# Moving the bulk transfers of an attention and MLP kernel from SyncE's queue to ScalarE's

## The chip, the cores and the metric

The kernel runs on one core of a Trainium2 chip. The core has TensorE (PE in the profile), VectorE (DVE), ScalarE (ACT), GpSimd (POOL) and SyncE (SP); each has its own instruction stream, worked off in order, and transfers between HBM and SBUF are issued as instructions in such a stream (SP's or ACT's here) and carried by 16 DMA engines. The metric is the device time of one launch in microseconds, as the median over runs.

## The reference

A layer of 2048 tokens of width 512, in float32: a layernorm without learned scale, from which an attention of 32 heads of 16 and a GELU MLP of width 1792 both read; their outputs and the input are added.

```python
xn = _layernorm(x)                                   # [1, 2048, 512]
qkv = (xn @ wqkv)                                    # 32 heads, Dh = 16
p = softmax(einsum("bhqd,bhkd->bhqk", q, k) * 16 ** -0.5)
a = einsum("bhqk,bhkd->bhqd", p, v).reshape(1, 2048, 512) @ wo
m = gelu(xn @ w1 + b1) @ w2 + b2                     # tanh form, F = 1792
return x + a + m
```

## The kernel before

**Units.** The attention is cut into 8 groups of 4 heads (NG) and 4 blocks of 512 queries (NQB), so 32 pairs t, and each pair into 16 units, one for each 128 keys. A unit is about 2.6 us long and does three things for different pairs: `s_half` makes four score tiles for a coming pair (PE, banks `pS`) whose row maxima DVE takes (L402); `e_half` makes four transposed score tiles of the present pair with the maxima folded in as two more rows of the product (PE, `pT`, three PSUM banks in turn), and ACT takes their exponentials into `pe` (L443, 12 buffers); `v_half` multiplies these with the values (PE, `pV`). There are 2048 exponentials. Between these products PE works on a list of background products (`dense`, banks `pD`): projections of values, queries and keys, then the MLP's two products, then the output projection. All of PE's products stand at one line of the program, L174.

**Stages.** The first 88 us are a start-up plan (layernorm, the first projections). From 88 to about 330 us the background is the rest of the projections, and GpSimd splits weights into pairs of float16 numbers, which are stored to HBM scratch. From about 330 to 1300 us it is the MLP in four blocks of 512 tokens, and then, to the end, the output projection.

**Transfers.** The background brings and keeps its data by transfers of its own: weight chunks in halves of 256 KB (`wch`, L887), columns for the projections (`wq`, L622); the normalised input `xt`, stored to scratch `xn_d` in 16 pieces (L1296) and read back as `xb`, 4 pieces for each block of the MLP (L709); the first MLP weight as 56 blocks `wc` of 256 KB (L714, three buffers, fetched two groups ahead); the second as 14 pieces into `w2_s` (L1425); and the partial sums `ac` (L1487). The attention has smaller ones, all on SP: stores of projected queries and keys (`qk_d`, L659 and L660), their loads as `kst` and `qst` (L565), the maxima as rows of `qst` (L360 and L364), and, at the end of each pair t, a chain for the sums of the softmax: `den_d` from `osb` (L494), back as `dn` (L497), its inverse to `den_d` (L504), spread as `rb` (L508), and the finished output `ot_d` (L520).

**What sets the order.** The program's order is the hardware's order on each of the five engines (`manual_schedule` with ORDERED). `later(n, fn, local, bulk)` puts a step in a queue that is due n ticks later; `tick`, called as the units go on, emits what is due. Steps with a size in `bulk` go through a lane that emits them at a limited rate:

```python
def run_lane(all_of_them=False):
    credit[0] = min(credit[0], 0) + LANE          # LANE = 225
    while lane and (all_of_them or credit[0] > 0 and not held[0]):
        size, fn = lane.pop(0)
        credit[0] -= size
        fn()
```

So the place of a transfer among all other instructions is the place in the program at which `fn` runs, whichever engine issues it. Each transfer counts up one of eight completion semaphores, taken in turn over all transfers of the program whatever engine issues them (DMAHW0 to DMAHW7 in the order below). Before it is issued its engine waits for the transfer eight back, which has the same semaphore, unless it is known to have landed; further waits are for data and for buffers.

Of the kernel before, what the change touches and what calls it, by code (L numbers as in the profile page):

```python
# [18 lines left out]
P = 128  # L19
S = 2048  # L20
D = 512
# [5 lines left out]
NF = F // P  # L27
QB = 512
# [16 lines left out]
WFROM, WSTEP, XN = 10, 4.5, 4.5  # L45
# [13 lines left out]
def layer_kernel(ctx: ExitStack, tc: tile.TileContext, x, wqkv, wo, w1, b1, w2, b2, out):  # L59
    nc = tc.nc  # L60
# [14 lines left out]
    xn_d = dram.tile([P, 2, NC, S], F16, name="xn_d")  # L75
    w1_d = dram.tile([NF // 2, P, 2, 2, NC, P], F16, name="w1_d")
    w2_d = dram.tile([P, 2, NF, D], F16, name="w2_d")
    acc_d = dram.tile([S, D], F32, name="acc_d")
# [143 lines left out]
    class Plan:  # L222
# [7 lines left out]
        def add(self, engine, ns, fn, after=(), take=(), free=(), size=0, tail=0, gap=0, small=False, lag=0):  # L230
            t = dict(gap=gap, small=small, lag=lag, e=engine, ns=ns, fn=fn, after=[a for a in after if a], take=take, free=free, size=size, tail=tail,
                     end=None, n=len(self.todo))
            for key in free:
                self.users.setdefault(key, []).append(t)
            self.todo.append(t)
            return t
# [66 lines left out]
    def later(n, fn, local=False, bulk=0):  # L303
        queue.append((slot[0] + n, fn, local, bulk))
# [262 lines left out]
    def stacks(g, w, blocks):  # L567
        for b in blocks:
            for a in range(2):
                stack(g, w, b, a)  # L570
# [45 lines left out]
    def load_qk(m):  # L616
        wf = []
        for w in range(2):
            wf.append(ph.tile([P, D], F32, name="wq", bufs=2).rearrange("p (c n) -> p c n", n=P))

            def load(w=w):
                nc.sync.dma_start(wf[w], wqkv[:, w * D + m * P:w * D + (m + 1) * P].rearrange("(c p) n -> p c n", p=P))  # L622
                here[m, w] = slot[0] + 4

            later(0, load, True, 256)
        return wf
# [12 lines left out]
    def by_slots(gen):  # L639

        def step():
            w = FINE
            while w == FINE:
                w = next(gen, 0)
            if w is None:
                later(1, step, True)

        later(1, step, True)
# [54 lines left out]
    feed, xbs, wcs = [], {}, {}  # L703

    def fetch_x(b):
        if b < NQB:
            xbs[b] = feed[0].tile([P, 2, NC, QB], F16, name="xb", bufs=1)
            for c in range(NC):
                later(1 + c, lambda c=c: nc.sync.dma_start(xbs[b][:, :, c], xn_d[:, :, c, b * QB:(b + 1) * QB]))  # L709

    def fetch_w1(n):
        if n < NQB * NF:
            wcs[n] = feed[0].tile([P, 2, NC, P], F16, name="wc", bufs=3)
            nc.sync.dma_start(wcs[n], w1_d[n % NF // 2, :, n % 2])  # L714

    def group(gen):

# [155 lines left out]
    with ExitStack() as st1:  # L873
# [3 lines left out]
        xt = ph.tile([P, 2, NC, S], F16, name="xt")  # L877
        xs = {}

        def chunk(src):  # L880
            wf = ph.tile([P, 4 * W], F32, name="wch", bufs=3)
            v = wf.rearrange("p (a b) -> p a b", b=src.shape[2])
            n = src.shape[1] // 2
            got = [v, 0, 0]

            def half(r):
                nc.sync.dma_start(v[:, r], src[:, r])  # L887
                got[1] += 1
                got[2] = pos[0] + 2

            for a in range(2):
                later(2, lambda r=slice(n * a, n * a + n): half(r), True, 256)
            return got
# [273 lines left out]
        for w in (1, 0):  # L1167
            wf, hi, lo, i1 = ("wq", 0, w), wqh[:, w, 0], wqh[:, w, 1], inv0[:, w:w + 1]
# [22 lines left out]
        for i in range(2):  # L1191
# [6 lines left out]
            else:  # L1198
                b = add("POOL", 1240, lambda key=key: nc.gpsimd.tensor_scalar(
                    tl[key], tl[key], inv_v[:, 0:1], 0.0, op0=ALU.mult, op1=ALU.add), [h])  # L1200
# [90 lines left out]
        def rest():  # L1291
            for k in range(8):
                later(8 + 4 * k, lambda k=k: stacks(1, 1 - k // 4, [k % 4]), True, 192)
            for k in range(4 * NQB):
                c, cols = k % 4, slice(k // 4 * QB, k // 4 * QB + QB)
                later(int(10 + XN * k), lambda c=c, cols=cols: nc.sync.dma_start(xn_d[:, :, c, cols], xt[:, :, c, cols]), True, 256)  # L1296
            for t in range(NV, NT):
                yield v_group(t, wvh, dbank)
            yield project(0, 0, NQB - 1, wqh, dbank)
            for m in range(1, 4):  # L1300
                while m not in ready_w:
                    yield None
                if m < 3:
                    by_slots(split_qk(m + 1, wfs[m + 1], inv1[0], ready_w))
                for sb in range(NQB):
                    for w in (1, 0):
                        yield project(m, w, sb, ready_w[m], dbank)
                    if m == 3 and sb == 2:
                        for n in range(2):
                            fetch_w1(n)  # L1310
                        fetch_x(0)
# [78 lines left out]
    def mlp():  # L1390
        m2 = st2p
        w2_s = m2.tile([P, 2, NF, D], F16, name="w2_s")
# [24 lines left out]
        for b in range(NQB):  # L1417
            xb = xbs[b]
            g = m2.tile([P, 2, NF, QB], F16, name="g", bufs=1)
            for f in range(NF):  # L1420
                later(1, lambda n=b * NF + f + 2: fetch_w1(n))
                wc = wcs[b * NF + f]
                if b == 0 and f >= 3:
                    for k in range(f - 3, NF if f == NF - 1 else f - 2):
                        later(2 * (k - f + 3), lambda k=k: nc.sync.dma_start(w2_s[:, :, k], w2_d[:, :, k]))  # L1425
                if b == 0 and f == 3:
                    nc.sync.dma_start(b2_b, b2[None, :].to_broadcast([P, D]))

                def hidden(hp, g=g, b=b, f=f):
                    hh = m2.tile([P, QB], F32, name="hh", bufs=3)  # L1430
                    bias = b1_s[:, f:f + 1]
                    if f % 2 == 0:
                        h_scale[0] = scale_reg(f"hs{f // 2 % 2}", fac1[0][0:1, f // 2:f // 2 + 1])
                    scale = h_scale[0]
                    nc.scalar.activation(hh, hp, AF.Identity, scale=scale, bias=bias)  # L1435
                    given("act", 700)
                    later(1, lambda: gelu(hh, g, b, f), True)

                yield Group([lambda c=c, i=i, j=j, wc=wc, xb=xb: (wc[:, i, c, :], xb[:, j, c, :])
                             for c in range(NC) for i, j in PAIRS], dbank, hidden, pace=FAST if f % 2 else SLOW)  # L1440
            for q in range(4):
                t = b * 4 + q
                xa = m2.tile([P, D], F32, name="xa", bufs=2)
                if q == 1:
                    fetch_x(b + 1)
                if b == NQB - 1 and q == 1:

                    ocs[2] = feed[0].tile([P, 2, NC, QB], F16, name="xb", bufs=1)
                    when((NG - 2) * NQB + 2, lambda: read_o(ocs[2], 2, True), 2)
                    for k in range(3):  # L1450
                        acs[8 + k] = feed[0].tile([P, D], F32, name="ac", tag="wc", bufs=3)
                        later(3 + k, lambda k=k: read_acc(acs[8 + k], 8 + k))
                nc.sync.dma_start(xa, x[t * P:(t + 1) * P, :])
                later(3, lambda xa=xa: pooled((1280, lambda: nc.gpsimd.tensor_tensor(xa, xa, b2_b, op=ALU.add))), True)

                def store(yp, xa=xa, t=t):
                    yt = m2.tile([P, D], F32, name="yt", bufs=2)
                    nc.scalar.activation(yt, yp, AF.Copy, scale=scale_reg("ys", gs[0:1, 2:3]))  # L1458
                    given("act", 600)
                    add = lambda: nc.gpsimd.tensor_tensor(xa, xa, yt, op=ALU.add)  # L1460
                    put = lambda: nc.sync.dma_start(acc_d[t * P:(t + 1) * P, :], xa)
                    later(1, lambda: pooled((1280, add), (0, lambda: later(4, put, True))), True)

                yield Group([lambda f=f, i=i, j=j, q=q, g=g: (g[:, i, f, q * P:(q + 1) * P], w2_s[:, j, f, :])
                             for f in range(NF) for i, j in PAIRS], dbank, store,
                            lambda n, b=b: (b, n // 3) in done, pace=FAST if b > 1 else MEAN)
# [17 lines left out]
        later(0, lambda: later(2, then), False, 1)  # L1484

    def read_acc(ac, t):
        later(0, lambda: nc.sync.dma_start(ac, acc_d[t * P:(t + 1) * P, :]), False, 256)  # L1487

    def finish(ac, t, store, *yos):
        put = lambda: nc.sync.dma_start(out[t * P:(t + 1) * P, :], ac)  # L1490
# [129 lines left out]
```

## Time and profile before

| | us |
|---|---|
| median of 3 runs | 1439.21 (1437.81 to 1444.19) |
| the profiled execution | 1438.07 |
| its span, first to last instruction | 1436.3 |
| DVE busy, mostly row maxima (L402, 1279.1) | 1346.9 |
| POOL busy | 693.4 |

The profile is of one execution; its time is 1.8 us above its span. A row of the page's groups gives the line of the program, the engine and operation, the tile written and the tile read, the count, the busy time and the mean duration, and what ended the engine's idle time ahead of it. A timeline row gives the start and length in us; a row with "x4" is four instructions of one kind in a run, and its length is that of the run. SPq and ACTq are transfers being issued, not the data moving. The granted TensorE clock was 1.000 over the span, and the transfers moved 87 GB/s in the mean.

### The profile page before, as it was taken

How to read it: one execution, taken by the hardware profiler on the slowest of the kernel's cores; microseconds unless marked ns; L12 is line 12 of the kernel's file. 1: busy time of each engine (PE TensorE's matmuls, PEld its weight loads, DVE VectorE, ACT ScalarE, POOL GpSimd, SP SyncE). 2: the span in 40 equal slices, each digit the busy share in tenths (PEclk: the TensorE clock that was granted, in tenths of full speed). 3: DMA queues.
4: the chain of work that ended last, by engine and by line, in shares of the span. 5: the costliest groups of instructions: out<-in, count | busy, mean ns of one | idle time of the engine just before them, and what ended most of it. 6: DMA issues, size and time to landing. Idle time of an engine off the chain costs nothing.

```text
span 1436.3 us, 88274 instructions
## 1 busy us (share of the span) xinstructions
PE 1423.7 (99%) x39979; PEld 969.1 (67%) x39979; DVE 1346.9 (94%) x2239; ACT 1253.5 (87%) x2389; POOL 693.4 (48%) x780
## 2 busy tenths in 40 slices
PE   8999999999999999999999999999999999999998
PEld 4657777666667777666667766676666667666665
DVE  8989999999999999999999999999999999999943
ACT  6678888889999888999988899998889998888886
POOL 6203866665687311478831157783026787202210
PEclk9999999999999999999999999999999999999999
DMA  7733556455224111221122011122112110212323
GB/s 233 225 114 97 162 158 206 158 172 148 85 65 128 60 27 27 64 76 43 38 59 75 25 51 45 52 71 60 38 32 77 57 39 19 60 56 78 109 73 116
DMA packets 110784, 124.95 MB, mean 87 GB/s; under 512 B 20812, under 2 KB 82252, under 8 KB 110408
## 3 DMA queue, kind: packets, MB, share of 16 engines
q1 hardware_dynamic: 103208, 109.87, 25.1%
q10 hardware_dynamic: 7200, 9.44, 2.2%
q8 instruction: 312, 5.11, 1.5%
q14 instruction: 64, 0.52, 0.1%
HBM read 81.79 MB, written 37.34 MB: 83 GB/s over the span
## 4 chain that ended last, share of the span: by engine, by line
PE 90%; DVE 5%; DMA 2%; issue 2%; ACT 1%; POOL 0%; SPq 0%; DVEq 0%; ACTq 0%; POOLq 0%
PE pD L174 28%; PE pV L174 26%; PE pT L174 19%; PE pS L174 16%; DVE mt L402 3%; DMA wch<-in_B_w_dram 1%; DMA pe<-in_A_x_dram 0%; DVE bs L1011 0%; DMA qk_d<-stg 0%; DMA wq<-in_A_wqkv_dram 0%; DMA wch<-in_A_wo_dram 0%; DVE ac L1493 0%; PE pD L1074 0%; ACT pe L443 0%; DVE wvh L1196 0%
## 5 line engine op out<-in xcount | busy, mean ns | idle before, releaser
L402 DVE TENSOR_REDUCE mt<-pS 128x1 f32<-128x512 f32 x2029 | 1279.1, 683 | 34.7 <-PE pS L174 8.2
L443 ACT ACTIVATE pe<-pT 128x512 f32<-128x512 f32 x2048 | 1109.4, 599 | 141.0 <-PE pT L174 60.2
L174 PE MATMUL pV<-pe,vv 64*32 64x512 f32 x8192 | 1086.6, 591 | 0.1
L174 PE MATMUL pT<-qst,kst 64*32 64x512 f16 x8192 | 703.4, 378 | 0.6 <-ACT vv L1212 0.3
L174 PE MATMUL pS<-kst,qst 62*32 62x512 f16 (+1 forms) x7945 | 627.0, 378 | 1.3 <-issue 0.8
L174 PEld LDWEIGHTS <-qst 62*32 62x32 f16 (+1 forms) x7964 | 309.9, 91 | 186.0 <-issue 34.1
L174 PE MATMUL pD<-xb,wc 64*32 64x512 f16 x5376 | 363.3, 375 | 0.0
L174 PE MATMUL pD<-w_s,g 64*32 64x512 f16 x5376 | 361.1, 375 | 0.0
L174 PEld LDWEIGHTS <-kst 64*32 64x32 f16 x8192 | 281.3, 91 | 98.5 <-issue 24.4
L174 PEld LDWEIGHTS pV<-pe,vv 64*32 64x32 f32 x8192 | 241.5, 105 | 11.0 <-PE pV L174 2.3
L174 PEld LDWEIGHTS <-wc 64*32 64x32 f16 x5376 | 160.4, 91 | 45.2 <-issue 0.3
L174 PEld LDWEIGHTS <-g 64*32 64x32 f16 x5376 | 162.6, 91 | 38.8 <-POOL g L1408 0.3
L174 PE MATMUL pD<-xt,wqk_h 64*32 64x512 f16 x2400 | 160.0, 376 | 0.1
L372 POOL TENSOR_SCALAR mparts<-mx 128x16 f16<-128x16 f32 x32 | 6.6, 206 | 294.3 <-DVE mx L370 284.6
L1460 POOL TENSOR_TENSOR xa<-xa,yt 128x512 f32<-128x512 f32 x16 | 20.6, 1284 | 167.8 <-ACT yt L1458 167.8
L174 PEld LDWEIGHTS <-wqk_h 64*32 64x32 f16 (+1 forms) x2448 | 78.2, 92 | 20.3 <-issue 1.0
L1414 POOL TENSOR_TENSOR t<-t,hh 128x512 f32<-128x512 f32 x56 | 71.9, 1284 | 4.7
L1407 POOL TENSOR_TENSOR t<-t,hh 128x512 f32<-128x512 f32 x56 | 71.8, 1283 | 4.5
L1412 POOL TENSOR_TENSOR t<-hh 128x512 f32<-128x512 f32 x56 | 58.3, 1041 | 21.3 <-ACT hh L1435 18.9
L1409 POOL TENSOR_TENSOR g<-t,g 128x512 f16<-128x512 f32 x56 | 65.2, 1165 | 4.7
L174 PE MATMUL pD<-wo_s,oc 64*32 64x512 f16 x912 | 61.0, 376 | 0.3 <-issue 0.3
L513 POOL TENSOR_TENSOR osb<-osb,rb 128x512 f32<-128x512 f32 x31 | 39.9, 1286 | 42.3 <-DMA rb<-den_d 29.0
(170 smaller groups left out, 942.1 us busy)
## 6 DMA issues: line engine op xcount, KB each, us to landing
wc<-w_d SPq DMA_DIRECT2D x56, 256.0 KB
qk_d<-stg SPq DMA_DIRECT2D x32, 256.0 KB
rb<-den_d SPq DMA_DIRECT2D x124, 64.0 KB
wch<-in_B_w_dram ACTq DMA_DIRECT2D x14, 512.0 KB
wch<-in_B_w_dram SPq DMA_DIRECT2D x28, 256.0 KB
w_d<-wsp SPq DMA_DIRECT2D x28, 256.0 KB
kst<-qk_d SPq DMA_DIRECT2D x64, 96.0 KB
qst<-qk_d SPq DMA_DIRECT2D x64, 96.0 KB
```

The source lines that it names most:

```text
L174: p = nc.tensor.matmul(*args, **kw)
L372: lambda: nc.gpsimd.tensor_scalar(parts[:, :, 0], mx[:, 0], 1.0 / MROW, 0.0, op0=ALU.mult, op1=ALU.add),
L402: nc.vector.reduce_max(mt_of[t][:, n // 2 + n % 2 * 2, qt, kb:kb + 1], s, axis=AX.X)
L443: nc.scalar.activation(pe, st, AF.Exp, scale=scale_of[g // 2])
L513: pooled((1280, lambda: nc.gpsimd.tensor_tensor(osb, osb, rb, op=ALU.mult)), (620, lambda: nc.gpsimd.tensor_scalar(ot[:, 0], osb, 1.0, 0.0 ...
L1407: (1280, lambda: nc.gpsimd.tensor_tensor(t1, t1, hh, op=ALU.mult)),
L1409: (1160, lambda: nc.gpsimd.tensor_tensor(g[:, 1, f, :], t1, g[:, 0, f, :], op=ALU.subtract)),
L1412: pooled((1040, lambda: nc.gpsimd.tensor_tensor(t1, hh, hh, op=ALU.mult)), (620, lambda: nc.gpsimd.tensor_scalar(t1, t1, 1.0, 1.0 / GELU_A ...
L1414: (1280, lambda: nc.gpsimd.tensor_tensor(t1, t1, hh, op=ALU.mult)),
L1460: add = lambda: nc.gpsimd.tensor_tensor(xa, xa, yt, op=ALU.add)
```

## The change

At seven lines the issuing engine becomes ScalarE; places in the program, sizes and buffers stay as they are.

```diff
@@ load_qk: load
-                nc.sync.dma_start(wf[w], wqkv[:, w * D + m * P:w * D + (m + 1) * P].rearrange("(c p) n -> p c n", p=P))
+                nc.scalar.dma_start(wf[w], wqkv[:, w * D + m * P:w * D + (m + 1) * P].rearrange("(c p) n -> p c n", p=P))
@@ fetch_x
-                later(1 + c, lambda c=c: nc.sync.dma_start(xbs[b][:, :, c], xn_d[:, :, c, b * QB:(b + 1) * QB]))
+                later(1 + c, lambda c=c: nc.scalar.dma_start(xbs[b][:, :, c], xn_d[:, :, c, b * QB:(b + 1) * QB]))
@@ fetch_w1
-            nc.sync.dma_start(wcs[n], w1_d[n % NF // 2, :, n % 2])
+            nc.scalar.dma_start(wcs[n], w1_d[n % NF // 2, :, n % 2])
@@ chunk: half
-                nc.sync.dma_start(v[:, r], src[:, r])
+                nc.scalar.dma_start(v[:, r], src[:, r])
@@ rest
-                later(int(10 + XN * k), lambda c=c, cols=cols: nc.sync.dma_start(xn_d[:, :, c, cols], xt[:, :, c, cols]), True, 256)
+                later(int(10 + XN * k), lambda c=c, cols=cols: nc.scalar.dma_start(xn_d[:, :, c, cols], xt[:, :, c, cols]), True, 256)
@@ mlp
-                        later(2 * (k - f + 3), lambda k=k: nc.sync.dma_start(w2_s[:, :, k], w2_d[:, :, k]))
+                        later(2 * (k - f + 3), lambda k=k: nc.scalar.dma_start(w2_s[:, :, k], w2_d[:, :, k]))
@@ read_acc
-        later(0, lambda: nc.sync.dma_start(ac, acc_d[t * P:(t + 1) * P, :]), False, 256)
+        later(0, lambda: nc.scalar.dma_start(ac, acc_d[t * P:(t + 1) * P, :]), False, 256)
```

These lines issue 154 of the program's 1013 transfers: 4 of `wq`, 16 of `xb`, 56 of `wc`, 32 of `wch`, 16 of `xn_d`, 14 of `w2_s` (named `w_s` in the profile) and 16 of `ac`. SP issues 841 after it and 995 before, ACT 172 and 18. The order of PE's, DVE's and POOL's instructions is the same.

The first place is where the first block of the MLP is brought in, 310 to 326 us in the profile before. On SP there stood, between loads of `wch` and `xb`, the store of the sums, the stores of projected keys, stores of split weights (`w_d`) and the finished output of a pair:

```order
L887 DMA wch<-in_A_wo_dram 128x512 x2
L709 DMA xb<-xn_d 128x2x512
L494 DMA den_d<-osb 1x512 x4
L659 DMA qk_d<-stg 128x2x512
L660 DMA qk_d<-stg 128x512
L1365 DMA w_d<-wsp 256x1x512
L709 DMA xb<-xn_d 128x2x512
L1365 DMA w_d<-wsp 256x1x512
L520 DMA ot_d<-ot 32x1x512 x4
L709 DMA xb<-xn_d 128x2x512
L497 DMA dn<-den_d 64x32
```

On ACT the same four loads of `xb` now stand among the exponentials, each with the semaphore that it waits for in brackets (the first is that of the fourth `den_d` store, the second that of the first `xb` load, the third that of the `dn` load, the fourth that of the L659 store behind the `dn` load):

```order
L443 ACTIVATE pe<-pT 128x512 [waits PE_49] x2
L709 DMA xb<-xn_d 128x2x512 [waits DMAHW7_49]
L443 ACTIVATE pe<-pT 128x512 [waits PE_49,Activation_49] x2
L443 ACTIVATE pe<-pT 128x512 [waits PE_49] x2
L709 DMA xb<-xn_d 128x2x512 [waits DMAHW7_49]
L443 ACTIVATE pe<-pT 128x512 [waits PE_49,Activation_49] x2
L672 ACTIVATE pf<-pD 128x512 [waits Pool_49]
L443 ACTIVATE pe<-pT 128x512 [waits PE_49] x2
L709 DMA xb<-xn_d 128x2x512 [waits DMAHW2_49]
L443 ACTIVATE pe<-pT 128x512 [waits PE_49,Activation_49] x2
L443 ACTIVATE pe<-pT 128x512 [waits PE_49] x2
L709 DMA xb<-xn_d 128x2x512 [waits DMAHW3_49]
```

The loads moved out from between SP's stores to between pairs of exponentials; of the stores around them nothing moved.

The second place is the third block of `wc`, 334 to 338 us before. On SP it stood between loads of keys (the number behind `kst` tells instances of the tile apart):

```order
 L504 DMA den_d<-dn 64x32
 L565 DMA kst_1_80<-qk_d 48x2x512 x2
-L714 DMA wc<-w_d 128x1024
 L565 DMA kst_2_81<-qk_d 48x2x512 x2
 L508 DMA rb<-den_d 32x512 x4
```

On ACT it has a row of its own among the exponentials, with the semaphore that the first of the two `kst_2_81` loads counts up:

```order
L443 ACTIVATE pe<-pT 128x512 [waits PE_49] x2
L443 ACTIVATE pe<-pT 128x512 [waits PE_49,Activation_49] x2
L443 ACTIVATE pe<-pT 128x512 [waits PE_49] x2
L714 DMA wc<-w_d 128x1024 [waits DMAHW3_49]
L443 ACTIVATE pe<-pT 128x512 [waits PE_49,Activation_49] x2
```

The block left SP's queue, where the loads of keys close up, for a place on ACT that is tied to one of these loads by its semaphore.

## The prediction

> **What bounds the kernel now.** I read the page first: the busy shares, the chain that ended last and the costliest groups.
>
> ```profile
> span 1436.3 us, 88274 instructions
> PE 1423.7 (99%) x39979; PEld 969.1 (67%) x39979; DVE 1346.9 (94%) x2239; ACT 1253.5 (87%) x2389; POOL 693.4 (48%) x780
> PE 90%; DVE 5%; DMA 2%; issue 2%; ACT 1%; POOL 0%; SPq 0%; DVEq 0%; ACTq 0%; POOLq 0%
> L443 ACT ACTIVATE pe<-pT 128x512 f32<-128x512 f32 x2048 | 1109.4, 599 | 141.0 <-PE pT L174 60.2
> ```
>
> PE is busy 99% of the span and makes up 90% of the chain. ACT has about 183 us of idle time (1436.3 − 1253.5), but the 2048 exponentials of L443 feed PE and take score banks back from it, so a stop of ACT is free only while PE can go on without the next exponential. What PE does not do in such a stop it cannot catch up. Next came the waits, on both ends of SP's queue:
>
> ```profile
> PEld L174 <- DMA qst<-qk_d: 1.3, 2, 1.0
> PEld L174 <- DMA qst<-m_d: 0.7, 1, 0.7
> SPq L360 <- ACT pe L443: 280.6, 30, 38.2
> SPq L714 <- PE pT L174: 31.4, 21, 5.2
> ```
>
> The columns are the total, the number and the longest wait. SP waits for long, but PE's waits for what SP brings come to 2.0 us (1.3 + 0.7). That is all that a freer SP can give PE.
>
> **What an issue costs on ACT.** Seven lines move 154 transfers. ACT already issues 18; one pair of these under an activation:
>
> ```profile
> 45.76 0.59 ACT L1061 ACTIVATE pf<-pT 128x512 f32<-128x512 f32 x1
> 45.76 0.93 ACTq L951 DMA_DIRECT2D wch<-in_B_w_dram  x2
> 46.23 0.60 ACT L1048 ACTIVATE xt<-pT 128x512 f16<-128x512 f32 x1
> ```
>
> Issues start with the activation that stands ahead of them and run beside it: two take 0.93 us, so one about 0.47, less than the 0.60 of an activation. A plain issue therefore costs PE nothing; its cover is the running exponential, and that cover is gone if the issue is long or has to wait.
>
> **The wait that comes with it.** In program order the transfers take eight completion semaphores in turn, and each waits, where it is not known already, until the one eight before has landed. This is no wait for data, and on SP it shows:
>
> ```profile
> 310.48 0.91 SPq L887 DMA_DIRECT2D wch<-in_A_wo_dram  x2
> 313.50 0.39 SPq L659 DMA_DIRECT2D qk_d<-stg  x1
> 316.37 0.34 SPq L660 DMA_DIRECT2D qk_d<-stg  x1
> SPq L660 <- DMA wch<-in_A_wo_dram: 2.5, 1, 2.5
> ```
>
> A store of q and k waits 2.5 us for a weight load with which it shares nothing; that load's second half, issued at about 310.9, landed at about 316.4, after 5.4 us. The short end of a landing is an ordinary head load:
>
> ```profile
> 26.70 0.78 SPq L565 DMA_DIRECT2D qst<-qk_d  x2
> 28.99 0.09 PEld L174 LDWEIGHTS <-qst 62*128 62x128 f16 x1 [0.95 <-DMA qst<-qk_d]
> ```
>
> That is 2.3 us from the issue to PE's waiting load. Moved transfers carry this wait to ACT, where everything behind it is exponentials, and behind those PE. The transfer waited for is often one of SP's, which by then stands *behind* other work in SP's own queue: on one queue the order made that wait short, on two it does not. How much PE can bear is the time from the end of an exponential to PE's next write of the same score bank (three banks in turn):
>
> ```profile
> 333.54 2.21 ACT L443 ACTIVATE pe<-pT 128x512 f32<-128x512 f32 x4 [0.18 <-PE pS L174]
> 334.44 0.40 PE L174 MATMUL pT<-qst,kst 64*32 64x512 f16 x4
> ```
>
> The first exponential of that row ends at 334.14 (333.54 + 0.60) and its bank is written at 334.44: 0.30 us of slack. So a place costs PE: predecessor's issue + landing + 0.4 for the issue itself − start of the next exponential − 0.3.
>
> **The four loads of xb (L709, 311 to 326 us).** The first goes out ahead of the exponentials of 315.06 and waits for the fourth den_d store; the second, ahead of 318.19, for the first xb load; the third, ahead of 320.96, for the load of dn.
>
> ```profile
> 311.43 0.59 SPq L709 DMA_DIRECT2D xb<-xn_d  x1
> 312.12 1.28 SPq L494 DMA_DIRECT2D den_d<-osb  x4
> 317.76 1.17 SPq L709 DMA_DIRECT2D xb<-xn_d  x1
> 315.06 1.08 ACT L443 ACTIVATE pe<-pT 128x512 f32<-128x512 f32 x2 [0.29 <-PE pS L174]
> 318.19 1.13 ACT L443 ACTIVATE pe<-pT 128x512 f32<-128x512 f32 x2 [0.29 <-PE pS L174]
> 320.96 1.09 ACT L443 ACTIVATE pe<-pT 128x512 f32<-128x512 f32 x2 [0.17 <-PE pT L174]
> 324.08 0.61 SPq L497 DMA_DIRECT2D dn<-den_d  x1
> ```
>
> First: the fourth store at 313.1 + 2.3 = 315.4, + 0.4 − 315.06 − 0.3 = 0.4. Second: issued at 315.4, landing 2.3 to 5.4 later, 0 to 2.7 (320.8 + 0.4 − 318.19 − 0.3). Third: 324.08 + 2.3 + 0.4 − 320.96 − 0.3 = 5.5, if SP were no earlier; rid of the moved issues ahead of it (0.91 at 310.48, 0.59 and 1.17 here, 2.7 in all) it is 2.8. These are clock times and not added: the longest counts, between 0.4 and 5.5. I take 3.0, the middle.
>
> **The third weight block (L714, 333 us).** It stands on ACT behind the four exponentials of 331.16 and waits for the first of two kst loads that SP issues after the place where this same wc load used to be:
>
> ```profile
> 331.16 2.21 ACT L443 ACTIVATE pe<-pT 128x512 f32<-128x512 f32 x4 [0.34 <-PE pS L174]
> 336.52 0.42 SPq L714 DMA_DIRECT2D wc<-w_d  x1
> 337.04 0.86 SPq L565 DMA_DIRECT2D kst<-qk_d  x2
> SPq L659 <- POOL stg L674: 1.9, 1, 1.9
> POOL stg L673 <- ACT pe L443: 3.6, 1, 3.6
> ```
>
> SP now reaches the load at 336.6 (337.04 − 0.42) and it lands at 338.9: 338.9 + 0.4 − 333.54 − 0.3 = 5.5. With the landing of 5.4 it is 8.6. SP has waited 1.9 us for POOL at 331.7, and POOL 3.6 us for ACT just before (both rows are of 318 to 346 us), so the stop of xb moves both on with it; if it does not, 5.5 − 3.0 = 2.5 is left. I take 4.5.
>
> **Two more weight blocks (L714, 441 and 1101 us).** Both stand between the second and third of four exponentials, and wait for the fourth ot_d store and the second kst load:
>
> ```profile
> 440.88 2.30 ACT L443 ACTIVATE pe<-pT 128x512 f32<-128x512 f32 x4
> 441.33 2.52 SPq L520 DMA_DIRECT2D ot_d<-ot  x4
> 1100.79 2.21 ACT L443 ACTIVATE pe<-pT 128x512 f32<-128x512 f32 x4
> 1100.95 1.66 SPq L565 DMA_DIRECT2D kst<-qk_d  x2
> ```
>
> At 441 the fourth store begins at 443.2 and lands at 445.5; the third exponential would begin at 442.0 (440.88 + 2 × 0.575): 445.5 + 0.4 − 442.0 − 0.3 = 3.6, or 3.2 if SP is 0.4 earlier. I take 3.3, between 3 and 6.7 (landing 5.4). At 1101 the second load begins at 1101.8, or 1101.3 without the wc issue ahead; 1103.6 + 0.4 − 1101.9 − 0.3 = 1.8. I take 1.7, between 1 and 5.
>
> **Stops among the weight chunks and xn_d stores (L887, L1296, L622, 117 to 308 us).** The largest:
>
> ```profile
> 272.41 1.30 SPq L1365 DMA_DIRECT2D w_d<-wsp  x2
> 273.03 1.08 ACT L443 ACTIVATE pe<-pT 128x512 f32<-128x512 f32 x2 [0.15 <-PE pT L174]
> ```
>
> A chunk ahead of 273.03 waits for the second w_d store (273.06): 275.4 + 0.4 − 273.03 − 0.3 = 2.5; SP loses a moved chunk and a moved store just ahead of it, which makes it 1.1. I take 1.7. Places like it at 130 to 183 us stand closer still to their predecessors: 0.8, between 0 and 4. The other wc loads, w2_s (L1425) and ac (L1487) wait for transfers issued 5 us and more ahead, which covers the landing: 0, and up to 2 if the landings are the long ones.
>
> **Long issues.** Some issues take far longer than 0.5 us on SP; of the moved lines 21 single ones take over 0.8 (the first and the last, and the spread of one line):
>
> ```profile
> 132.73 0.91 SPq L1296 DMA_DIRECT2D xn_d<-xt  x1
> 1331.13 1.42 SPq L1487 DMA_DIRECT2D ac<-acc_d  x1
> L714 SPq DMA_DIRECT2D wc<-w_d x56: 320/372/1866, 308.7 to 1170.0; - x56
> ```
>
> Under a cover of 0.60 + 0.3, 1.42 us costs 0.5 and 0.91 nothing, 0.25 in the mean; with those in pairs about 30 of them give 7.5. If they belong to SP's queue and not to the chip, 0, as ACT's pair above. I take 2.0: the ACT rows are the nearer, but were taken before the stage with the traffic.
>
> **The sum.** 3.0 + 4.5 + 3.3 + 1.7 + 1.7 + 0.8 + 0 + 2.0 = 17.0; SP's relief gives back 1.0 of the 2.0 that PE waits: +16.0. From the profiled run, 1438.07 (its span 1436.3 and 1.8 around it), this is 1454.1; that run lies 1.1 below the median of 1439.21, on which it makes 1455.2. I predict **1455**. The low ends give 0.4 + 2.5 + 3 + 1 + 1.1 + 0 + 0 − 2.0 = +6.0 (1445), the high ends 5.5 + 8.6 + 6.7 + 5 + 2.5 + 4 + 2 + 7.5 = +42 (1481), but not all at once.
>
> **Rivals.** *Hidden after all.* SP, rid of 154 issues, sends the predecessors early enough, and ACT's idle time swallows the rest. For it: SP's waits are long, ACT's share is 87%. Against it: the wc load at 333 needs a predecessor issued by 331, and SP is held until 331.7 by POOL. What stays is one or two places, +0 to +5: about 1441. [...]
>
> *Faster.* The queue that carries the head loads and the softmax sums no longer stands behind bulk: wc alone made SP wait 31.4 us for PE, with kst and qst loads behind it. If these loads also set the dense work's order in time, PE gains its 2.0 us of waits and part of the 2% that the chain shows as DMA, most of it before 88 us where nothing moves. That is −2, and past −7 only if PE's idle time of 12.6 us (1436.3 − 1423.7) were mostly SP's; it decides only where no stop of ACT exceeds 0.9 us. About 1436. [...]
>
> *Long issues fall on ACT as on SP.* The same stops, and 7.5 instead of 2.0: 1461, and with long landings up to 1475.
>
> *The change does not do what it says.* The moved transfers wait for no engine by data, but their semaphores tie them to SP's; that is the forecast's own ground, not a fourth time.
>
> **How the numbers follow.** Stops of ACT with mostly covered issues (1446 to 1460): 0.52; with long issues or landings (above 1460): 0.28; hidden: 0.15; faster rival: 0.05. A measurement of this kernel tells a difference from 0.5%, 7.2 us, on. Of the faster case most lies within that: faster 0.03. Same takes the hidden case, the rest of the faster one, and little of the first: 0.18. Slower: 0.79. The range leaves out half of the small cases and the far end of the long ones: 1442 to 1472.
>
> **What would show it.** Right: in the changed profile ACT's exponentials wait for a DMA, or stand idle before the row behind a DMA row, by 2 to 6 us at 314 to 323, 333, 441 and 1101, and PE has gaps as long at the same places; PE's busy time stays near 1424 us while the span grows. The xn_d, w2_s and ac issues show no gap over 1 us. ACT's issues at and over 1 us number few. Wrong: no gap of PE over 1 us between 117 and 1300, or many small gaps behind issues without a wait (then the issue itself was mis-sized), or gaps in the last stage behind ac.

## The result and the profile after

The changed kernel took 1462.97 us in the median (1458.11 to 1469.48) against 1439.53 us: 23.4 us more, a ratio of 1.0169 with a 95% interval of 1.0149 to 1.0189. It is slower, as forecast (1455, 1442 to 1472), by 8 us more than the number said. The profiled execution, 1458.11 us, is the shortest of the four.

The page of the changed kernel: span, busy shares and the chain that ended last.

```profile
span 1456.3 us, 88248 instructions
PE 1431.3 (98%) x39979; PEld 967.5 (66%) x39979; DVE 1347.3 (93%) x2239; ACT 1251.8 (86%) x2389; POOL 692.3 (48%) x780
PE 85%; DVE 5%; DMA 4%; issue 2%; POOL 2%; ACT 1%; SPq 1%; ACTq 0%; DVEq 0%; POOLq 0%
```

Two things moved. The span is 20.0 us longer, and PE is busy 7.6 us longer (1431.3 − 1423.7) for the same 39979 products. The list of waits has rows that were not there before (total, number, longest):

```profile
PE pT L174 <- ACT pe L443: 12.2, 10, 4.6
ACT pe L443 <- DMA kst<-qk_d: 9.3, 3, 5.3
ACT pe L443 <- DMA xb<-xn_d: 1.9, 1, 1.9
ACT pe L443 <- DMA w_d<-wsp: 1.7, 1, 1.7
ACT pe L443 <- DMA qst<-m_d: 1.4, 1, 1.4
ACT pe L443 <- DMA dn<-den_d: 1.3, 1, 1.3
```

An exponential reads `pT` and writes `pe`; it has no data in common with a load of keys. Yet ACT's exponentials waited for transfers, SP's in all but one row, 15.6 us in the rows above, and PE waited 12.2 us for exponentials. 12.2 and the 7.6 of more busy time make 19.8 of the 20.0 us. The largest place is the one forecast, the third block of wc; ACT, SP and PE there:

```profile
336.99 2.21 ACT L443 ACTIVATE pe<-pT 128x512 f32<-128x512 f32 x4 [0.34 <-PE pS L174]
344.06 0.34 ACTq L714 DMA_DIRECT2D wc<-w_d  x1
344.51 2.06 ACT L443 ACTIVATE pe<-pT 128x512 f32<-128x512 f32 x4 [5.30 <-DMA kst<-qk_d]
...
339.63 2.87 SPq L565 DMA_DIRECT2D kst<-qk_d  x4
...
339.30 0.61 PE L174 MATMUL pD<-xb,wc 64*32 64x512 f16 x8
...
345.15 0.62 PE L174 MATMUL pT<-qst,kst 64*32 64x512 f16 x4 [4.58 <-ACT pe L443]
...
345.53 1.09 PE L174 MATMUL pD<-xb,wc 64*32 64x512 f16 x8
```

ACT ends its fourth exponential at 339.2 and stands until the wc transfer goes out at 344.06. The transfer it waits for is the third of SP's four kst loads from 339.63 on, which goes out at 340.7. PE follows with a gap of 4.58 us. Then eight products take 1.09 us where they took 0.61 before the stop. The windows say why (the number behind the window's length is PE's busy time, the last three columns are the granted clock, the DMA share and GB/s); below them are those of the second longest gap, 2.31 us, which ends at 1121.7:

```profile
342.00:344.00 2.00, 0.00 (x0) 0.00 (x0) 0.00 (x0) 0.00 (x0) 0.00 (x0) 0.80 0.44 132
344.00:346.00 2.00, 0.85 (x16) 0.43 (x23) 0.00 (x0) 1.49 (x4) 0.00 (x0) 0.50 0.60 183
346.00:348.00 2.00, 2.00 (x44) 1.18 (x36) 0.42 (x1) 0.98 (x3) 0.00 (x0) 0.50 0.47 152
348.00:350.00 2.00, 2.00 (x40) 1.11 (x32) 0.87 (x2) 0.80 (x3) 0.00 (x0) 0.50 0.00 0
350.00:352.00 2.00, 2.00 (x72) 1.24 (x60) 1.92 (x4) 1.68 (x4) 0.00 (x0) 1.00 0.03 8
...
1120.00:1122.00 2.00, 0.30 (x8) 0.21 (x15) 0.58 (x1) 0.95 (x2) 1.47 (x2) 0.86 0.63 147
1122.00:1124.00 2.00, 2.00 (x40) 1.09 (x32) 0.00 (x0) 1.11 (x3) 0.00 (x0) 0.50 0.83 264
1124.00:1126.00 2.00, 2.00 (x59) 1.13 (x43) 1.29 (x2) 1.45 (x3) 0.00 (x0) 0.79 0.40 124
```

During the first stop the granted TensorE clock falls to 0.50 and stays there for some 5 us after PE has begun again, and the second ends the same way. These two stops of PE are paid twice: the stop itself, and products at half speed behind it. The windows say how much: PE worked 4.85 us at half clock behind the first (0.85 + 2 + 2) and some 3.1 behind the second (0.30 + 2 + 0.84, where 0.84 is the part of the last window at half clock, (1 − 0.79) × 2 / 0.5), in all 8.0 us. Half of that, 4.0 us, is the estimate of what is lost. In every other window with PE at work the clock is 1.00, so 3.6 of the 7.6 us have another cause. Part of them can be the ordinary spread of PE's busy time, which is 1422.3 to 1423.7 us in the profiles of kernels without a stop; the rest stays open.

### The profile page after: what moved, and what is told of

It reads as the page before. It is cut to its first block, busy times and chain, and to the rows that moved or that the text cites. A ratio compares the mean times of both kernels' runs of the same rounds, so it can differ in the third digit from the quotient of the medians.

```text
span 1456.3 us, 88248 instructions
## 1 busy us (share of the span) xinstructions
PE 1431.3 (98%) x39979; PEld 967.5 (66%) x39979; DVE 1347.3 (93%) x2239; ACT 1251.8 (86%) x2389; POOL 692.3 (48%) x780
## 4 chain that ended last, share of the span: by engine, by line
PE 85%; DVE 5%; DMA 4%; issue 2%; POOL 2%; ACT 1%; SPq 1%; ACTq 0%; DVEq 0%; POOLq 0%
PE pD L174 26%; PE pV L174 25%; PE pT L174 19%; PE pS L174 15%; DVE mt L402 3%; DMA kst<-qk_d 1%; DMA wch<-in_B_w_dram 1%; ACT pe L443 1%; DMA m_d<-mturned 1%; DMA pe<-in_A_x_dram 0%; DMA wq<-in_A_wqkv_dram 0%; DVE bs L1011 0%; SPq L520 0%; DMA w_d<-wsp 0%; DMA qk_d<-stg 0%
## 5 line engine op out<-in xcount | busy, mean ns | idle before, releaser
L174 PE MATMUL pT<-qst,kst 64*32 64x512 f16 x8192 | 703.7, 379 | 13.0 <-ACT pe L443 12.2
```

Of the source, the lines that this page charges most:

```text
L174: p = nc.tensor.matmul(*args, **kw)
```

## The experiments

Theory: the cost lies in a few moved transfers that hold ACT by their semaphore wait for a transfer still standing in SP's queue. First rival: each issue on ACT costs its share, 23.4/154 = 0.15 us. Second rival: a transfer's own cost (its data, its traffic) is what matters, not the wait. Third: SP's relief is worth something, which the stops hide.

### The lines apart

Only `fetch_w1` changed:

```diff
-            nc.sync.dma_start(wcs[n], w1_d[n % NF // 2, :, n % 2])
+            nc.scalar.dma_start(wcs[n], w1_d[n % NF // 2, :, n % 2])
```

> Only the 56 loads of wc (L714) go to ScalarE's queue, the other six lines stay on SyncE. Theory (a few transfers stop the exponentials by their semaphore wait for a transfer of SyncE, and PE stops behind them): the stops at the third block (333 us before, 7.1 us of delay in the changed kernel), at 1101 us (4.1) and at 441 us (1.5) stay, those of the other lines are gone: 10 to 15 us slower than before, with one gap of PE over 3 us near 340 and one over 1.5 us near 1110. Rival (every issue on ScalarE costs its share, 23.4 us / 154 = 0.15 us): 56 x 0.15 = 8.5 us slower, spread evenly, with no single gap.

Measured: 1453.03 against 1438.39 us, ratio 1.0112 (1.0094 to 1.0130), 14.6 us. PE shows gaps of 4.65 us at 336, 1.39 at 451 and 2.55 at 1113 behind exponentials, and 0.67 and 0.91 at 316 and 470, which wait for none. The three are single gaps where they were expected.

Everything changed but that line:

```diff
 # L622, L709, L887, L1296, L1425, L1487: nc.scalar.dma_start
 # L714 stays:
             nc.sync.dma_start(wcs[n], w1_d[n % NF // 2, :, n % 2])
```

> The other six lines (98 transfers) go to ScalarE's queue, wc stays on SyncE. Theory of single semaphore waits: what the changed kernel lost at 256 to 266 us (2.5), 312 to 318 us (1.9) and in small steps before (1 to 2) stays, nothing at 333, 441 and 1101: 3 to 8 us slower. Rival of a cost for each issue: 98 x 0.15 = 15 us slower.

Measured: 1448.37 us, ratio 1.0072 (1.0052 to 1.0092): 10.0 us, above the 3 to 8 of the theory and below the 15 of the rival. Its gaps are few again (0.72 us at 159, 1.33 at 265, 3.62 at 278, 1.55 and 1.17 at 325 to 331), and none lies behind 331. Up to 308 us this program and the changed kernel are the same, and yet the gap at 278 was 3.62 us here and 0.52 there. So the size of a stop can differ much between executions of the same instructions; that it is set by how the two queues stand to each other in that execution is my reading, which no run tests.

Lines L1425 and L1487 alone:

```diff
-                        later(2 * (k - f + 3), lambda k=k: nc.sync.dma_start(w2_s[:, :, k], w2_d[:, :, k]))
+                        later(2 * (k - f + 3), lambda k=k: nc.scalar.dma_start(w2_s[:, :, k], w2_d[:, :, k]))
...
-        later(0, lambda: nc.sync.dma_start(ac, acc_d[t * P:(t + 1) * P, :]), False, 256)
+        later(0, lambda: nc.scalar.dma_start(ac, acc_d[t * P:(t + 1) * P, :]), False, 256)
```

> Only the second weight (L1425, 14 transfers) and the partial sums (L1487, 16) go to ScalarE's queue. Theory of single semaphore waits: their predecessors landed 5 us and more before, so nothing stops: 0 (-1 to +1). Rival of a cost for each issue: 30 x 0.15 = 4.6 us slower. Rival that issues on ScalarE are long where they were long on SyncE: some exponentials start 0.3 to 1 us late, 0 to 2 us slower.

Measured: 1437.08 us, ratio 0.9993 (0.9983 to 1.0003). Thirty transfers cost nothing, where the first rival expected 4.6 us.

Then three more single lines. L709 alone:

```diff
-                later(1 + c, lambda c=c: nc.sync.dma_start(xbs[b][:, :, c], xn_d[:, :, c, b * QB:(b + 1) * QB]))
+                later(1 + c, lambda c=c: nc.scalar.dma_start(xbs[b][:, :, c], xn_d[:, :, c, b * QB:(b + 1) * QB]))
```

> Only the 16 xb loads (L709) go to ScalarE's queue. Theory of single semaphore waits: the four loads at 311 to 326 us wait for transfers of SyncE and for one another, 2 to 5 us slower with gaps of PE of 1 to 2 us there; the other twelve cost nothing. Rival of a cost for each issue: 16 x 0.15 = 2.4 us, of which three quarters at 480 us and later.

Measured: ratio 1.0039 (1.0024 to 1.0053), 5.1 us in the medians. ACT there:

```profile
316.97 0.61 ACTq L709 DMA_DIRECT2D xb<-xn_d  x1
317.69 2.06 ACT L443 ACTIVATE pe<-pT 128x512 f32<-128x512 f32 x4 [3.40 <-DMA qk_d<-stg]
321.35 0.53 ACTq L709 DMA_DIRECT2D xb<-xn_d  x1
322.27 1.08 ACT L443 ACTIVATE pe<-pT 128x512 f32<-128x512 f32 x2 [2.52 <-DMA ot_d<-ot]
```

The first two xb loads hold ACT. Of the 2.9 us that PE waited for exponentials in this execution 2.5 lie between 308 and 335 us; 0.4 are left for the rest of the span, with the twelve loads of later blocks.

L887 and L622 alone, and L1296 alone:

```diff
-                nc.sync.dma_start(v[:, r], src[:, r])
+                nc.scalar.dma_start(v[:, r], src[:, r])
... (and the load of wq in load_qk); in the second kernel only:
-                later(int(10 + XN * k), lambda c=c, cols=cols: nc.sync.dma_start(xn_d[:, :, c, cols], xt[:, :, c, cols]), True, 256)
+                later(int(10 + XN * k), lambda c=c, cols=cols: nc.scalar.dma_start(xn_d[:, :, c, cols], xt[:, :, c, cols]), True, 256)
```

> Only the weight chunks (L887, 32 transfers) and the columns for the projections (L622, 4) go to ScalarE's queue. Theory of single semaphore waits: chunk loads at 258 to 281 us wait for stores of SyncE just issued (q and k, split weights), with gaps of PE of 1 to 3.5 us there and some under 1 us at 130 to 185: 2 to 6 us slower. Rival of a cost for each issue: 36 x 0.15 = 5.4 us, in small steps from 130 to 311 us, without gaps over 1 us.

> Only the 16 stores of xn_d (L1296) go to ScalarE's queue; all lie between 117 and 309 us. Theory of single semaphore waits: few of them find a transfer of SyncE issued under 3 us before, 0 to 2 us slower. Rival of a cost for each issue: 16 x 0.15 = 2.4 us.

Measured: 1447.16 against 1436.97 us, ratio 1.0071 (1.0054 to 1.0088), for the chunks, and 1444.67, ratio 1.0045 (1.0031 to 1.0059), for the stores. These are 10.2 and 7.7 us, where 2 to 6 and 0 to 2 were expected: the places were right, the sizes and the stop of the stores were not. The largest stop of each, on ACT, first of the chunks and then of the stores:

```profile
281.04 0.33 ACTq L887 DMA_DIRECT2D wch<-in_B_w_dram  x1
281.43 2.06 ACT L443 ACTIVATE pe<-pT 128x512 f32<-128x512 f32 x4 [4.62 <-DMA w_d<-wsp]
```

```profile
147.79 0.52 ACTq L1296 DMA_DIRECT2D xn_d<-xt  x1
148.42 2.06 ACT L443 ACTIVATE pe<-pT 128x512 f32<-128x512 f32 x4 [3.92 <-DMA kst<-qk_d]
```

The stop at 148 does not occur in the changed kernel, where its place has no gap of PE over 0.35 us. The parts, 1.12, 0.39, 0.71, 0.45 and −0.07%, add up to 2.6%, the whole is 1.69%. The excess is not in wc: wc alone (1.12) and everything else (0.72) make 1.84%, which the intervals do not tell from 1.69. It is in the other six lines, whose four parts make 1.48% apart and 0.72% together. A reading that fits: what is moved alone leaves SP's queue full, and its predecessors late; what is moved together takes work out of SP's queue, and the predecessors of one line leave earlier because another line is gone. No kernel here changed the queue's length alone, so this is not shown.

### One transfer, and when it is reached

A single transfer of the 154, the third block of wc:

```diff
-            nc.sync.dma_start(wcs[n], w1_d[n % NF // 2, :, n % 2])
+            (nc.scalar if n == 2 else nc.sync).dma_start(wcs[n], w1_d[n % NF // 2, :, n % 2])
```

> One single transfer of the 154 goes to ScalarE's queue: the third block of wc (n = 2, 336.5 us in the profile before). Theory of single semaphore waits: ScalarE waits for the kst load that follows on SyncE; delay of 5 to 8 us, of which 3 to 5 as one gap of PE and the rest as products at a lower granted clock behind it. Rival of a cost for each issue: 0.15 us, no gap. Rival that SyncE's relief makes up for single waits: 0.

Measured: 1445.83 us against 1438.39, ratio 1.0061 (1.0041 to 1.0081). One transfer of 256 KB costs 7.4 us in the medians. The waits between 326 and 346 us:

```profile
ACT pe L443 <- DMA kst<-qk_d: 5.1, 1, 5.1
PE pT L174 <- ACT pe L443: 4.4, 1, 4.4
```

The same transfer, one and then two units later on ACT. SP's instructions, the order of all transfers and the one waited for are the same in the three kernels:

```diff
-                later(1, lambda n=b * NF + f + 2: fetch_w1(n))
+                later(2 if b + f == 0 else 1, lambda n=b * NF + f + 2: fetch_w1(n))    # 3 in the second
```

> As the kernel with the third block of wc alone on ScalarE's queue, but this block is issued one unit later: two groups of exponentials (2.4 us) further on ScalarE, with SyncE's instructions and the transfer that it waits for the same. Theory of the semaphore wait: ScalarE's wait of 5.1 us becomes 2.7, PE's gap of 4.4 us about 2.0, and with the products at a lower clock behind it 3 to 4.5 us slower than before, against 7.4 there. Rival that the transfer itself or its issue on ScalarE costs the time: 7.4 as there.

> The same block two units later (4.8 us further on ScalarE). Theory of the semaphore wait: the kst load has landed or is within 0.3 us of it, no gap of PE, 0 to 0.5 us slower than before. Rival that the transfer or its issue costs the time: 7.4.

Measured: ratio 1.0022 (1.0013 to 1.0031), 3.3 us in the medians, for one unit, and 1.0005 (0.9997 to 1.0014), 1.0 us, for two. The same two rows of the waits, of the first and then of the second kernel:

```profile
ACT pe L443 <- DMA kst<-qk_d: 3.1, 1, 3.1
PE pT L174 <- ACT pe L443: 2.4, 1, 2.4
```

```profile
ACT pe L443 <- DMA kst<-qk_d: 1.0, 1, 1.0
PE pT L174 <- ACT pe L443: 0.5, 1, 0.5
```

ACT's wait falls 5.1, 3.1, 1.0 as the place moves by 2.4 us each time, PE's stop 4.4, 2.4, 0.5, and the time 7.4, 3.3, 1.0. In each, PE bears 0.5 to 0.7 us of ACT's wait. (The last time, 1.0, is not clear of the noise.) The engine, the issue, the bytes and the semaphore are the same in the three; only the place differs, and with it the wait. So it is the wait that costs, and the second rival falls.

### All that does not stop

```diff
-            nc.sync.dma_start(wcs[n], w1_d[n % NF // 2, :, n % 2])
+            (nc.sync if n in (0, 1, 2, 14, 15, 47) else nc.scalar).dma_start(wcs[n], w1_d[n % NF // 2, :, n % 2])
-                later(1 + c, lambda c=c: nc.sync.dma_start(xbs[b][:, :, c], xn_d[:, :, c, b * QB:(b + 1) * QB]))
+                later(1 + c, lambda c=c: (nc.scalar if b else nc.sync).dma_start(xbs[b][:, :, c], xn_d[:, :, c, b * QB:(b + 1) * QB]))
 # L1425 and L1487: nc.scalar; L622, L887 and L1296 stay on nc.sync
```

> 92 of the 154 transfers go to ScalarE's queue: w2_s, ac, the xb loads of the last three blocks and 50 of the 56 wc loads (not the six at 308 to 337, 439 to 449 and 1100 us). Those left on SyncE are the ones at whose place the changed kernel stops. Theory of single semaphore waits: -1 to +2 us against before, no gap of PE over 1 us between 100 and 1400 us. Rival of a cost for each issue: 92 x 0.15 = 14 us slower. Rival that SyncE's relief is worth something: 2 us faster or more.

Measured: 1436.50 against 1437.58 us, ratio 0.9998 (0.9988 to 1.0008), which is −1.7 to +1.1 us. What PE still waited for exponentials:

```profile
PE pT L174 <- ACT pe L443: 0.3, 1, 0.3
```

92 transfers on ACT's queue cost at most 1.1 us, not 14, and SP's relief from 92 gains less than 2. Both the first and the third rival fall here.

## Why the prediction was right, and what was mis-sized

**The mechanism** was the forecast one: an issue on ACT cost nothing that shows (92 of them at most 1.1 us), the semaphore wait in front of it did, and PE stopped with ACT. The single block (5.1 us of wait, 4.4 of stop) and the same block issued later (1.0 and 0.5) show it with only the place changed. Of the signs that the forecast named, gaps of 2 us and more came at two of the four places, and PE's busy time did not stay near 1424 us.

**The places.** Gaps of PE in the changed kernel stand at 341 us (4.58; forecast 4.5), at 1119 (2.31; forecast 1.7) and 456 (1.03; forecast 3.3), and at 323 behind the xb loads (1.27; forecast 3.0). Earlier ones are 0.46, 1.12 and 0.52 at 175, 265 and 278 (forecast 2.5 together). They sum to 11.3 us (12.2 with the gaps under 0.45 us), against 15.0 in the forecast (17.0 less the 2.0 for long issues). Among the xb loads the working had the third as the longest; the second was (1.9 us of ACT's wait, in the row for `xb`), and the third stopped PE for 0.34 us. PE also bore 0.5 to 0.7 us of a wait, not the 0.30 of the working.

**The term that was missing** is PE's longer busy time, 7.6 us. The sum counted what PE stands, and not that PE ran at half clock, 0.50, behind two of the stops (4.0 us of the 7.6, by the estimate above). The stops came out 2.8 us smaller than forecast, the long issues 2.0 smaller and SP's relief 1.0 smaller, and the busy time put 7.6 on: in the profiled run the change cost 20.0 us against a sum of 16.0. That the errors nearly cancel is luck. The median is 3.4 us further off than the profiled run, the shortest of four. The other three executions had mean granted clocks of 0.996, 0.995 and 0.992, the lowest in the longest of them, which suggests more time at half clock there; no profile shows it. At 1463 the median lies in the class that the forecast gave to long issues or landings (above 1460, 0.28): the issues were not long, and half clock was in no class. The gaps of PE behind which it came, and one behind which it did not, stand in the last section.

**Long issues**, 2.0 us, were 0. The durations of L714's issues on ACT (shortest, median, longest, in ns), and in the kernel without stops its fifty on ACT:

```profile
L714 ACTq DMA_DIRECT2D wc<-w_d x56: 326/331/515, 313.7 to 1192.6; - x56
```

```profile
L714 ACTq DMA_DIRECT2D wc<-w_d x50: 326/331/362, 341.2 to 1170.4; - x50
```

On SP they took up to 1866 ns. Of all seven lines the longest issue on ACT in the changed kernel was 0.81 us (L887), still under the forecast's cover of 0.9. The long issues stayed with SP's queue (in the kernel without stops its six issues of L714 took 0.37 to 1.62 us), and the prediction's rival of long issues on ACT fell.

**SP's relief**, −1.0, did not show. PE's two rows of waits for what SP brings came to 2.0 us before (1.3 and 0.7), and in the changed kernel they are:

```profile
PEld L174 <- DMA qst<-qk_d: 1.3, 2, 0.9
PEld L174 <- DMA qst<-m_d: 0.7, 1, 0.7
```

The time of the 92 moved transfers (−1.7 to +1.1 us) cannot tell 1.0 from 0. The rival of a faster kernel fell, and so did that of a hidden cost, which needed the waits to be over before ACT came to them.

**The block at 341 and the one at 456.** The working for the first gave 5.5, and 4.5 was taken in case SP did not move on with the stop of xb. SP's load went out at 340.7, 4.1 us later than the working's 336.6, and ACT came 5.7 us later (339.2 against 333.54), so SP had moved with most of it; and the load took 3.3 us to land (344.06 less 340.7), not 2.3. With these the working gives 340.7 + 3.3 + 0.4 − 339.2 − 0.3 = 4.9, and 4.58 was measured. That 4.5 was so near is again two errors that cancel. At 456 the distance itself was wrong: SP's ot_d stores were taken at their distance of before, but they began only 10.8 us later than before (441.33), while the exponentials of 440.88 began 12.9 us later, at 453.80. ACT so came 2.1 us nearer to the landing, and of the 3.3 some 1.2 is left; 1.03 was measured:

```profile
452.15 2.57 SPq L520 DMA_DIRECT2D ot_d<-ot  x4
```

## What to carry to other kernels

Before a transfer is moved to another engine's queue, write down what it waits for in the new order, completion semaphores included, and where that transfer stands in its own queue; "waits for no other engine" is a statement on data alone. To an engine that feeds a saturated PE, move only those transfers whose predecessors have landed when the engine comes to them: 92 at places without a stop cost at most 1.1 us here. Where one has not, issue it later: here two units later left 1.0 us of 7.4, one unit 3.3. No kernel here gave ACT's transfers completion semaphores of their own, so whether that ends the waits is not shown. Sum PE's waits on the old queue first: PE was 99% busy here and they came to 2.0 us, so taking load off that queue had at most these 2 us to give.

## What the runs showed of the hardware

The clock after short stops was not expected. In these kernels gaps of PE of 1.0 to 1.55 us left the granted clock at 1.00, and gaps of 2.12 us (xb alone), 2.31 and more were followed by a clock of 0.50, with one exception, a gap of 2.35 us: the block one unit later, PE's products behind the gap and two windows.

```profile
338.23 0.40 PE L174 MATMUL pT<-qst,kst 64*32 64x512 f16 x4 [2.35 <-ACT pe L443]
...
338.45 0.61 PE L174 MATMUL pD<-xb,wc 64*32 64x512 f16 x8
...
337.00:339.00 2.00, 0.77 (x24) 0.57 (x31) 0.22 (x1) 1.42 (x3) 0.00 (x0) 1.00 0.58 192
339.00:341.00 2.00, 2.00 (x72) 1.39 (x59) 1.29 (x2) 2.00 (x5) 0.00 (x0) 1.00 0.51 166
```

So of two stops a little over 2 us one brought the half clock (2.12) and one did not (2.35). Once there, it lasted 6.8 us at 343 in the changed kernel (by the windows of the result 0.8 + 2 + 2 + 2) and 3.4 us at 1121 (0.56 + 2 + 0.84). In the five kernels with some of the lines moved that show it, every such stretch lasted 3.4 us, and behind the single block 6.8. The gap alone does not set it: 4.65 us (wc alone) brought 3.4 us of half clock, and 4.4 (the single block) 6.8. What sets it is not shown. That stretches of half clock differ so may be a second reason, beside the standing of the queues, why executions of one kernel spread over 11 us (1458.11 to 1469.48). An issue of the same wc transfer took 0.33 us on ACT in the median and at most 0.52, and 0.37 and up to 1.87 on SP; why SP's queue has the long ones stays open.
